# Attention and a gated feed-forward layer on one core: all probability-times-value products from the sixth pair on in 64x64 tiles, one drain copy per pair, a new order

## The chip, the cores and the metric

The kernel runs on one core of one Trainium2 chip. The metric is the device time of one execution in microseconds, lower is better. Three runs of the kernel before gave 418.28 us (median; 417.99 to 421.44). One execution was profiled: it took 417.28 us, of which 415.5 us lie between the start of its first and the end of its last profiled instruction (the span).

## The reference

```python
# q, k, v: (8, 12, 448, 64) float32; tau = 0.1
q_n = q / (norm(q, axis=-1) + 1e-6);  k_n = k / (norm(k, axis=-1) + 1e-6)
scores = q_n @ k_n.T / tau
attn = exp(scores - max(scores));  attn = attn / (sum(attn) + 1e-9)
x = (attn @ v).transpose(0, 2, 1, 3).reshape(8 * 448, 12 * 64)
# w_in: (768, 2048), w_out: (2048, 768)
h = x @ w_in
out = (h * cos(h)) @ w_out                   # (3584, 768) float32
```

## The kernel before, in words

**Work.** There are 8 batches of 12 heads. Two heads make a pair `g` (48 pairs, 6 to a batch), three pairs a unit `u`. For each pair the raw q and k rows are loaded by SyncE's queue, squared (`square`), summed over the head (`reduce`), turned into inverse norms (`rnorm`), scaled to bf16 (`scale`) and transposed (`transposes`, by TensorE for the first nine pairs, by DMA later). No maximum is taken out of the scores: cosine scores over tau are bounded.

**Scores.** `scores(g, c)` makes the transposed scores, keys on partitions, in 64x64 tiles of TensorE: 448 keys are seven blocks of 64, so block `c = 0` is half as wide (224 columns per matmul) and `c = 1, 2, 3` hold two blocks each (448 columns). ScalarE's exponential writes them in bf16 to `PH` (c = 0) and `PX` (c = 1 to 3).

**Gather.** `attend(g)` multiplies these probabilities by v and by ones (for the sums of the softmax) into one of three PSUM buffers (`AV`, `SC0`, `SC1`). It has two forms. The common form uses tiles of 128 rows by 32 columns: 12 matmuls of 448 columns at L979 (`av`), 4 of 224 at L1004 (`sm2`), 4 to 12 of 224 at L996 (`sm`), and the half block in 64x64 tiles at L972 (`row`). The other form, for the seven pairs listed in `PLAN["quarters"]` (7 to 11, 17 and 23), uses 64x64 tiles only: `run_phase` (L1015, `phase`) runs through the keys twice, once per diagonal of the tiles, each step being four matmuls of 224 columns in the four quadrants at once, and `ends` (L1024) does the half block. VectorE may first add `PX` blocks together (`FO`, "fold", L933), so that fewer matmuls with ones are needed; `folds(g)` says how many.

**Normalising.** For the pairs in `PLAN["direct"]` ScalarE makes exp(-ln(sum)) and GpSimd multiplies (L1077). For the others two copies drain the buffer (L1110 by VectorE, L1107 by ScalarE: 128x224 sums, then 128x448 values), and per unit `chain(u)` gathers the sums by DMA (`sums<-xu`), takes the reciprocal on VectorE (L1156), writes it to HBM (`scr<-rcp`), reads it back to all partitions (`RB<-scr`) and lets GpSimd multiply (L1163). The result `xT` is the transposed input of the next layer. The drained values stand in a ring of three units.

**Feed-forward layer.** Per batch `m1(b)` makes 16 blocks of h in 128x128 tiles (L1178); for each two blocks ScalarE takes the cosine (L1209) and VectorE multiplies (L1211) into `gT`. `m2_quarters` makes the output in rows of 128 with 64x64 tiles (L1278), the last ones `m2_fill` with 128x128 tiles (L1307). VectorE drains them (L1245).

**Order.** Everything is recorded as operations with reads and writes (`Program.op`); `arrange` plans all engines with estimated costs, per-operation biases (`PLAN["bias"]`) and, for TensorE, the order written out in `PLAN["order"]`. `PLAN["script"]` says when each score block (`s`), half block (`a`, `b`), values (`c`), first diagonal (`d`), batch (`m`) and filling of output work (`f`) is recorded. On the chip each engine then works through its own list in order and waits on semaphores. `P.settled(first, then)` marks an accumulation that must wait until an earlier matmul into the same columns has been written.

Of the kernel before, what the change touches and what calls it, by code (L numbers as in the profile page):

```python
# [6 lines left out]
ACT = mybir.ActivationFunctionType  # L7
# [11 lines left out]
    "vector": (20, 22, 24, 26, 32, 38, 40, 44, 46),  # L19
    "fold": 1,  # L20
    "folds": {6: 2, 8: 2, 10: 0, 12: 0, 16: 2, 17: 1, 18: 2, 20: 2, 21: 2, 22: 2, 24: 2, 25: 2, 26: 2, 27: 2, 30: 2,
# [12 lines left out]
    "v3": (7, ("xa", 2, 0)),  # L34
    "late4": {2: (7, "T9")},
    "power": (2,),
    "late": {6: 7.5, 9: 1.0, 11: 2.5, 13: 1.5},
# [10 lines left out]
    "scaled": {},  # L48
    "squared": {(5, 2): "A"},
# [5 lines left out]
    "direct": (0, 1, 2, 3, 4, 5, 7, 8, 9, 10, 11, 17, 23, 47),  # L55
# [196 lines left out]
class Program:  # L252
# [12 lines left out]
    LANDING = 0.45  # L265
    BOTH = 1.09
    COLD = 2.7
    ROOM = 2200

    def __init__(self, new_sem):  # L270
        self.new_sem = new_sem
# [8 lines left out]
    def op(self, eng, fn, reads=(), writes=(), cost=0.0, mode=None, dma=None, bulk=0.0, lock=False, label="", bias=0.0):  # L280
        o = Op()
# [1277 lines left out]
```

## Time and profile before

| What | us | Share of the span |
|---|---|---|
| Profiled execution | 417.28 | |
| Its span | 415.5 | |
| TensorE matmuls (PE) | 402.9 | 97% |
| Weight loads (PEld, beside PE) | 247.4 | 60% |
| VectorE (DVE) | 247.5 | 60% |
| ScalarE (ACT) | 261.7 | 63% |
| GpSimd (POOL) | 243.3 | 59% |

A busy time is the union of an engine's instructions. Matmuls overlap and their ends are modelled, so in the timeline the distance from one group's start to the next group's start tells what a group costs, not its length. "PE L1015 ... x4" is a group of four matmuls of line 1015.

### The profile page before, as it was taken

The numbers are of one execution on the slowest core, as the hardware profiler recorded it, in microseconds if no ns is written. First come the engines' busy times: TensorE is split into PE (matmuls) and PEld (weight loads), VectorE is DVE, ScalarE is ACT, GpSimd is POOL, SyncE is SP. The second block draws the span as 40 slices with busy tenths as digits, with TensorE's granted clock in tenths as the row PEclk, the third lists the DMA queues.
The fourth block names the chain that finished last, engine by engine and source line by source line (L and its number), as shares of the span: only waits on it lengthen the run. The fifth ranks groups of instructions, "written<-read, shape, count | busy, mean of one in ns | idle before, by whom it ended". The sixth has DMA issues, their size and how long they took to land.

```text
span 415.5 us, 13714 instructions
## 1 busy us (share of the span) xinstructions
PE 402.9 (97%) x6096; PEld 247.4 (60%) x6096; DVE 247.5 (60%) x350; ACT 261.7 (63%) x366; POOL 243.3 (59%) x192
## 2 busy tenths in 40 slices
PE   7899998999999999999899999999999999999997
PEld 3454556865667656765466657675566656655565
DVE  4564766357786598777674478454886555414412
ACT  5887577895888636876387656765486755413500
POOL 4999976799656675778657358816878300230000
PEclk9999999999999999999999999999999999999999
DMA  8999999869969998759945991989974800430114
GB/s 194 258 256 226 209 216 188 198 138 202 171 112 171 202 242 162 110 138 162 254 92 109 213 256 25 182 131 225 233 136 83 185 4 5 109 96 24 39 38 115
DMA packets 78591, 63.50 MB, mean 153 GB/s; under 512 B 43332, under 2 KB 73540, under 8 KB 78532
## 3 DMA queue, kind: packets, MB, share of 16 engines
q1 hardware_dynamic: 60324, 49.94, 57.7%
q0 software_dynamic: 18048, 12.59, 20.7%
q8 instruction: 48, 0.79, 0.8%
q10 hardware_dynamic: 160, 0.10, 0.1%
q14 instruction: 11, 0.09, 0.1%
HBM read 54.98 MB, written 11.13 MB: 159 GB/s over the span
## 4 chain that ended last, share of the span: by engine, by line
PE 86%; DMA 6%; POOL 3%; DVE 2%; ACT 1%; issue 1%; SPq 1%; DVEq 0%; POOLq 0%
PE MP L1278 26%; PE SC L1178 19%; PE AV L1178 9%; PE SC L914 5%; PE MP L1178 4%; PE MP L1307 4%; PE SC L979 3%; PE SC L1307 3%; PE AV L979 2%; DMA sums<-xu 2%; PE AV L1015 2%; DMA RB<-scr 1%; DMA scr<-rcp 1%; PE AV L914 1%; POOL qks L860 1%; DMA raw<-in_q_dram 1%
## 5 line engine op out<-in xcount | busy, mean ns | idle before, releaser
L1278 PE MATMUL MP<-W,gT 64*64 64x384 bf16 x2816 | 138.1, 323 | 1.8 <-issue 1.3
L929 ACT ACTIVATE PX<-SC 128x896 bf16<-128x896 f32 x115 | 102.4, 916 | 18.1 <-PE SC L914 17.0
L1278 PEld LDWEIGHTS MP<-W,gT 64*64 64x64 bf16 x2816 | 90.5, 107 | 25.5 <-issue 3.0
L860 POOL TENSOR_TENSOR qks<-raw,rn 128x896 bf16<-128x896 f32 (+1 forms) x48 | 80.2, 1680 | 26.1 <-ACT rn L852 16.5
L1178 PE MATMUL SC<-xT,W 128*128 128x448 bf16 x456 | 92.7, 353 | 1.8 <-DVE gT L1211 1.8
L822 POOL TENSOR_TENSOR sq<-raw 128x896 bf16<-128x896 f32 x44 | 73.6, 1684 | 20.8 <-DVE n L829 11.8
L1163 POOL TENSOR_TENSOR xT<-xu,RB 128x448 bf16<-128x448 f32 x34 | 38.0, 1136 | 66.8 <-DMA RB<-scr 47.1
L1178 PEld LDWEIGHTS SC<-xT,W 128*128 128x128 bf16 x456 | 44.0, 98 | 44.3 <-issue 3.2
L1209 ACT ACTIVATE cosb<-SC,cst 128x896 f32<-128x896 f32 x38 | 38.1, 1006 | 40.2 <-PE SC L1178 36.0
L829 DVE TENSOR_REDUCE n<-sq 128x14 f32<-128x896 bf16 (+2 forms) x49 | 51.3, 1056 | 4.5 <-ACT sq L820 4.1
L1211 DVE TENSOR_TENSOR gT<-SC,cosb 128x896 bf16<-128x896 f32 x38 | 41.1, 1086 | 20.4 <-ACT cosb L1209 17.9
L933 DVE TENSOR_TENSOR FO<-PX 128x896 bf16<-128x896 bf16 x39 | 37.8, 968 | 25.6 <-ACT PX L929 25.4
L1178 PE MATMUL AV<-xT,W 128*128 128x448 bf16 x228 | 47.7, 352 | 0.6 <-POOL xT L1163 0.6
L914 PE MATMUL SC<-qkT 64*64 64x448 bf16 x460 | 41.9, 357 | 0.6 <-ACT PX L929 0.4
L1209 ACT ACTIVATE cosb<-AV,cst 128x896 f32<-128x896 f32 x19 | 19.1, 1007 | 36.5 <-PE AV L1178 35.1
L1245 DVE COPY osb<-MP 128x384 f32<-128x384 f32 x50 | 25.8, 552 | 19.5 <-PE MP L1278 14.7
L1178 PEld LDWEIGHTS AV<-xT,W 128*128 128x128 bf16 x228 | 22.1, 98 | 21.4 <-ACT PX L929 1.1
L1211 DVE TENSOR_TENSOR gT<-AV,cosb 128x896 bf16<-128x896 f32 x19 | 20.7, 1090 | 22.5 <-ACT cosb L1209 22.5
L929 ACT ACTIVATE PX<-AV 128x896 bf16<-128x896 f32 x29 | 26.7, 920 | 6.2 <-PE AV L914 6.2
L796 POOL DMA_DIRECT2D va<-in_v_dram x32 | 21.8, 690 | 6.7 <-DMA raw<-in_q_dram 4.1
L929 ACT ACTIVATE PH<-SC 128x448 bf16<-128x448 f32 x37 | 20.2, 546 | 6.3 <-PE SC L922 5.3
L933 DVE TENSOR_TENSOR FO<-FO,PX 128x896 bf16<-128x896 bf16 x25 | 18.7, 749 | 6.4 <-ACT PX L929 5.4
(119 smaller groups left out, 470.3 us busy)
## 6 DMA issues: line engine op xcount, KB each, us to landing
raw<-in_k_dram SPq DMA_DIRECT2D x48, 224.0 KB, 6.3
raw<-in_q_dram SPq DMA_DIRECT2D x48, 224.0 KB, 7.1
out_dram<-osb SPq DMA_DIRECT2D x54, 192.0 KB, 3.4
va<-in_v_dram POOLq DMA_DIRECT2D x32, 192.0 KB, 7.1
RB<-scr SPq DMA_DIRECT2D x18, 336.0 KB, 4.9
W<-in_moe_w_in_dram POOLq DMA_DIRECT2D x4, 768.0 KB, 13.4
W<-in_moe_w_out_dram POOLq DMA_DIRECT2D x4, 768.0 KB, 16.3
RB<-scr SPq DMA_DIRECT2D x6, 224.0 KB, 3.5
```

The lines of the kernel that those rows point to most:

```text
L822: pool(lambda e, x=x, y=y: e.tensor_tensor(y, x, x, ALU.mult), src_, dst, 0.1 + n * 1.78e-3, label="sq%d.%d" % (u, p)).pad = LATE if u > 1 ...
L829: dve(lambda e, w=w: e.tensor_reduce(out=n2v[i][:, 2 * p : 2 * p + 2, w], in_=sqv[p][:, :, w, :], axis=mybir.AxisListType.X, op=ALU.add), ...
L860: f = lambda e, s0=s0, s1=s1: e.tensor_tensor(qksv[i][:, p, s0:s1].rearrange("p s h d -> p h s d"), rawv[i][:, h, s0:s1, :], bass.AP(rn[i] ...
L914: m = e.matmul(ph[BP * o : BP * o + BP, a, 0:S], t[r, c - 1 + (NT3 + 1) * o, 0:BP], t[r, :, BP : 2 * BP], start=True, stop=True)
L929: act(lambda e: e.activation(PHv[g % 3] if c == 0 else PXv[j][:, c - 1], ph[:, :, 0:n], ACT.Exp, scale=1.0 / TAU), keys, [("PX", j, c) if ...
L933: dve(lambda e: e.tensor_tensor(FO[j].ap(), x, PXv[j][:, c - 1].rearrange("p a s -> p (a s)"), ALU.add), [("PX", j, c), ("PX", j, 1) if c ...
L1163: f = lambda e, p=p: e.tensor_tensor(xTv[b % 2][:, UP * i + p, :].rearrange("p (s o m) -> p s o m", s=NB, o=2), xuv[:, u % 3, p, :].rearra ...
L1178: t = e.matmul(ph[:, a, 0:S], W1v[:, order[c], 128 * n : 128 * n + 128], xTv[b % 2][:, order[c], :], start=(c == 0), stop=(c == NKC - 1))
L1209: act(lambda e, ph=ph, cz=cz: e.activation(cosv[cz], ph[:, :, 0:S], ACT.Sin, bias=cst.ap()[:, 0:1], scale=1.0), names(gi) + ["cst0"], [("c ...
L1211: dve(lambda e, ph=ph, cz=cz, gi=gi: e.tensor_tensor(gTv[:, 2 * gi : 2 * gi + 2, S * (b % 2) : S * (b % 2) + S], ph[:, :, 0:S], cosv[cz], ...
L1278: r = e.matmul(POH[b][x : x + 64, 0:HW], gTv[k, y, col + x : col + x + 64], W2v[k, y, HW * b : HW * b + HW], start=(y == 0 and h == 0), st ...
L1307: r = e.matmul(po[:, 0 : w[1] - w[0]], gTv[:, y, col : col + 128], W2v[:, y, w[0] : w[1]], start=(y == 0), stop=(y == NF - 1))
```

## The change

- Pairs 6 to 47 all use the 64x64 form. The tile forms of L972, L979 (from pair 6 on), L996 and L1004 go.
- The query halves of a score block now stand swapped for 64 of the 128 rows (the moving operand is read with another stride), so that the two diagonals read contiguous halves.
- Where `tailed(g)`, VectorE also adds the half block `PH` onto `FO`, and the ones part of `ends` goes.
- One copy of 128x896 drains a non-direct pair, by ScalarE for the pairs in `acts`, else by VectorE; the ring has two units instead of three; `gather`, `spread` and the reciprocal work on 96x28 instead of 128x21.
- Two diagonals may run in either order with the half block (`dac` or `adc`); every step of the first half is the one that the second half must settle behind.
- ScalarE takes 13 more of the squares and 17 output drains (`oacts`); VectorE takes three scalings and three multiplications (`fast`); pair 35 becomes direct.
- The planner gets a model of TensorE's instruction fetch, output tiles are recorded per batch (`m2_upto`), all biases, delays, the order and the script are new.

```diff
-    "quarters": (7, 8, 9, 10, 11, 17, 23),
+    "quarters": (6, 7, 8, ..., 47),
-    "fold": 1,
+    "fold": 2,
+    "tailed": 1,
-    "late": {6: 7.5, 9: 1.0, 11: 2.5, 13: 1.5},
+    "late": {2: 3.5, 4: 3.0, 5: 3.0, 6: 5, 7: 3.0, 8: 5.0, 9: 3.0, 10: 3.0, 11: 3.5, 12: 3.5, 13: 3.0, 14: 3.0, 15: 1.0},
-    "grain": 4,
-    "fast": (),
+    "grain": 2,
+    "fast": (27, 33, 42),
...
@@ scores
+                    x = t[r, :, BP : 2 * BP]
+                    if g >= PB:
+                        x = bass.AP(qkT[y], 64 * a * 2 * S + BP + HQ * o, [[2 * S, 64], [HQ - 2 * HQ * o, 2], [2 * BP, NB], [1, HQ]])
+                    m = e.matmul(ph[BP * o : BP * o + BP, a, 0:S], t[r, c - 1 + (NT3 + 1) * o, 0:BP], x, start=True, stop=True)
...
+        if g >= PB and tailed(g) and c == 1 + folds(g):
+            xt = FO[j].ap().rearrange("p (a s) -> p a s", a=2)[:, :, 0:SH]
+            dve(lambda e: e.tensor_tensor(xt, xt, PHv[g % 3], ALU.add), [("F", j), ("PH", g % 3)], [("F", j)], SH, lock=True,
+                label="tail%d" % g, bias=PLAN["bf"][1])
@@ attend
-                    m = e.matmul(av_[64 * a : 64 * a + 64, b, x], w, source(kind, c)[r, a, :, b, :], start=(h == 0 and c == 0 and kind == "V"),
+                    m = e.matmul(av_[64 * a : 64 * a + 64, b, x], w, source(kind, c)[r, a, SH * h : SH * h + SH], start=(h == 0 and c == 0 and kind == "V" and not swapped),
...
                 if h and n == 0:
                     P.settled(opened[g], o)
+                opened[g] = o
...
-                    for k in range(2):
+                    for k in range(1 if tailed(g) else 2):
                         opened[g] = P.op("PE", lambda e, k=k: ends(e, k), ...
...
+            slot = slotv[:, i, p]
+            if not direct:
+                to, src_ = slot.rearrange("p x (h s) -> p h x s", h=2), av_[:, :, 0:S].rearrange("p h (x s) -> p h x s", x=2)
+                if g in PLAN["acts"]:
+                    act(lambda e: e.activation(to, src_, ACT.Copy, bias=0.0), both_keys, [("xa", i, p)], 2 * S, label="xu%d" % g)
+                else:
+                    dve(lambda e: e.tensor_copy(to, src_), both_keys, [("xa", i, p)], 2 * S, label="xu%d" % g)
+                return
...
@@ chain
-        dma("SP", [lambda e: e.dma_start(sums[i].ap()[:, 0:w], bass.AP(xu, XS[i], [[32 * XW, 4], [w, 32], [1, w]]))],
-            [("xs", i, p) for p in range(n)], [("sums", i)], "sums%d" % i, 0.35,
+        dma("SP", [lambda e: e.dma_start(sums[i].ap()[0:rows, :],
+                                         bass.AP(xu, i * UP * 2 * S + UP * S, [[64 * XW, 2], [w, 16 * n], [1, w]]))],
+            [("xa", i, p) for p in range(n)], [("sums", i)], "sums%d" % i, 0.35,
...
@@ m2_drain
-        if ends and w[1] == DM:
+        if ends and w[1] == DM or (t, hf) in PLAN["oacts"]:
@@ new
+    def m2_upto(n):
+        while m2_queue and m2_queue[0][0] < n:
+            t = m2_queue[0][0]
+            banks[0], nhalf[0] = [(["PO"], PO), (["TP"], TPF)], 0
+            while m2_tile or m2_queue and m2_queue[0][0] == t:
+                m2_fill(2 if t in PLAN["flat"] else 2 * NF, t not in PLAN["flat"])
@@ Program.play, for a TensorE operation: blocks of 256 instructions, asked for some 50 before an edge
+                        asked += self.BLOCK
+                        usable[asked] = t + self.FETCH + min(self.SHARE * behind, 5.5)
...
+                        o.end += max(0.0, usable[edge] - t)
```

More of the change, by code (lines that the diff above doesn't have):

```diff
@@ L248 @@
     __slots__ = ("eng", "fn", "idx", "deps", "cost", "mode", "dma", "bulk", "lock", "label", "bias",
-                 "start", "end", "late", "weight", "guard", "pad", "descs", "lead", "free", "waits", "inc", "count", "pos", "dcount", "known", "nd")
+                 "start", "end", "late", "weight", "guard", "pad", "descs", "lead", "free", "waits", "inc", "count", "pos", "dcount", "known", "nd", "ins")
 class Program:
@@ L306, in order_only @@
     def order_only(self, first, then):
+        assert first.eng == then.eng
         then.deps.append((first, None))
@@ L940, in folds, with tailed @@
         return PLAN["folds"].get(g, PLAN["fold"])
+    def tailed(g):
+        return folds(g) and PLAN["tails"].get(g, PLAN["tailed"])
     opened, held, turned = {}, {}, set()
@@ L965, in rest @@
                     m = e.matmul(to, w, PHv[g % 3][r, a, :],
[L966 to L973 removed]
+                                 start=(n == 0), stop=False)
             return m
@@ L979, in av @@
                 t = e.matmul(av_[o : o + 32, 0, 0:S], vav[y][:, 2 * p + a, c + 1, d : d + 32], PXv[j][:, c, a, :],
-                             start=(c == 0 and swapped), stop=(c == NT3 - 1 and not swapped))
+                             start=False, stop=(c == NT3 - 1))
             return t
```

338 lines of the change are left out of this document (155 added, 183 removed), and 268 rows, old and new, of the table PLAN.

## The prediction

> **What bounds the kernel now.** I read the page first, then the timeline of TensorE around the instructions that go, then counts per line, then the waits. The page:
>
> ```profile
> span 415.5 us, 13714 instructions
> ...
> PE 402.9 (97%) x6096; PEld 247.4 (60%) x6096; DVE 247.5 (60%) x350; ACT 261.7 (63%) x366; POOL 243.3 (59%) x192
> ...
> q8 instruction: 48, 0.79, 0.8%
> ...
> PE 86%; DMA 6%; POOL 3%; DVE 2%; ACT 1%; issue 1%; SPq 1%; DVEq 0%; POOLq 0%
> ```
>
> TensorE is idle 12.6 us in all and holds 86% of the chain that ended last; every other engine is busy for under two thirds. So an edit is worth what it does to TensorE's list: columns, changes of tile shape, and waits. The execution took 417.28 us, 1.8 more than its span. I keep that 1.8 and make the sum against 417.28; the median of the runs, 418.28, lies 1.0 above it.
>
> Where the idle time lies shows in four stretches (columns: length, then busy time of PE, PEld, DVE, ACT, POOL with counts, clock, DMA share and GB/s):
>
> ```profile
> 0.00:34.00 34.00, 29.74 (x352) 14.70 (x353) 19.75 (x37) 26.54 (x51) 28.60 (x30) 1.00 1.08 236
> ...
> 55.00:87.20 32.20, 29.57 (x768) 22.89 (x769) 16.55 (x29) 27.57 (x44) 23.14 (x18) 1.00 1.00 193
> ...
> 105.40:143.90 38.50, 37.87 (x922) 25.69 (x922) 26.96 (x46) 32.13 (x46) 22.52 (x17) 1.00 0.96 160
> ...
> 188.40:208.70 20.30, 18.48 (x104) 9.22 (x104) 14.00 (x16) 10.00 (x10) 14.64 (x11) 1.00 1.23 207
> ```
>
> 4.3, 2.6, 0.6 and 1.8 us of TensorE's idle time are here: the start, and 5.1 us in three places behind it. The rest of the kernel is columns back to back at the full clock (1.00).
>
> **Tile shapes.** This is the timeline of TensorE around one pair in the old form (start, length, group):
>
> ```profile
> 60.43 0.38 PE L914 MATMUL SC<-qkT 64*64 64x448 bf16 x4
> 60.74 0.75 PE L979 MATMUL AV<-PX,va 128*32 128x448 bf16 x12
> 61.32 0.27 PE L1004 MATMUL AV<-PH,half 128*32 128x224 bf16 x4
> 61.42 0.27 PE L996 MATMUL AV<-FO,ones 128*32 128x224 bf16 x4
> 61.62 0.60 PE L914 MATMUL SC<-qkT 64*64 64x448 bf16 x8
> ```
>
> And a pair in the new form:
>
> ```profile
> 65.07 0.27 PE L1015 MATMUL AV<-PX,va 64*64 64x224 bf16 x4
> 65.17 0.27 PE L1015 MATMUL AV<-FO,ones 64*64 64x224 bf16 x4
> 65.26 0.27 PE L1015 MATMUL AV<-PX,ones 64*64 64x224 bf16 x4
> 65.36 0.27 PE L1024 MATMUL AV<-PH,va 64*64 64x224 bf16 x4
> 65.45 0.27 PE L1024 MATMUL AV<-PH,ones 64*64 64x224 bf16 x4
> 65.79 0.48 PE L1015 MATMUL AV<-PX,va 64*64 64x224 bf16 x12
> ...
> 66.30 0.36 PE L914 MATMUL SC<-qkT 64*64 64x448 bf16 x4
> 66.48 0.33 PE L1278 MATMUL MP<-W,gT 64*64 64x384 bf16 x4
> ```
>
> Start to start, a group of four with 224 columns costs 0.095 to 0.10 in either shape (65.07 to 65.45 in four steps; 61.32 to 61.42); I take 0.096. A score group of 448 columns costs 0.18 (66.30 to 66.48), one of L979 0.193 (60.74 to 61.32 in three). Going from the score group into the 32-wide shape took 0.31, so 0.12 is the change; coming back took 0.20 from L996, so 0.10. A change costs 0.11 on average.
>
> The old form's counts after the first five pairs, in the windows view restricted to one line each: L979, L996, L1004, L972, L1015, L1024, in this order (the number in brackets):
>
> ```profile
> 55.00:415.50 360.50, 26.54 (x420) 1.00 0.74 141
> 55.00:415.50 360.50, 9.95 (x180) 1.00 0.74 141
> 55.00:415.50 360.50, 9.20 (x136) 1.00 0.74 141
> 55.00:415.50 360.50, 17.82 (x136) 1.00 0.74 141
> 55.00:415.50 360.50, 11.14 (x280) 1.00 0.74 141
> 55.00:415.50 360.50, 2.96 (x56) 1.00 0.74 141
> ```
>
> With 8 and 12 more of pair 47 that is 796 matmuls of 224 columns, 199 groups, and 432 of 448, 108 groups: 199 x 0.096 + 108 x 0.193 = 39.9 us. The changed program has 1488 of the two diagonals and 248 of the half block, all of 224 columns: 434 groups, 41.7 us. **Columns: +1.8.** The form is not cheaper in itself: each sum with ones is made twice over half of the keys. Without the deeper folds (66 additions and 22 tails instead of 64 additions) it would be more still.
>
> Along the two instruction orders TensorE changes its shape 102 times before and 56 times after. **Shapes: -46 x 0.11 = -5.1.** By 0.10 and 0.12 per change the ends are -4.6 and -5.5.
>
> A rule speaks against small groups: the Trainium skill's "TensorE: Matmul & The Clock Gate" (Part 1, on the 56 ns gap) says that starts of matmuls never come closer than about 25 ns, however few the columns. By it 434 groups would take 43.4 us and the sum would end 1.7 later; the trace (0.095 per four, 24 ns each) stands a little below that floor, and the sum goes by the trace.
>
> **Settling.** The second half must wait until the first is written. Where nothing stands between, 65.45 to 65.79 took 0.34 instead of 0.096: 0.24 per place. In the new order the second half follows directly in 7 pairs (6, 8, 22, 29, 30, 41, 47), and with one group of 0.1 between in 4 more; before in one. **+6 x 0.24 + 4 x 0.1 = +1.9**; at least 0 where the wait was due anyway, at most 0.24 for each of 21 pairs with under 0.2 us between, +5.
>
> **Output work.** 128 matmuls of L1278 (32 groups) become 32 of L1307's kind, 384 columns either way: 0.
>
> **Waits that may go.** The largest in the middle of the kernel are these:
>
> ```profile
> 142.98 0.27 PE L996 MATMUL SC<-FO,ones 128*32 128x224 bf16 x4
> 143.87 0.35 PE L1178 MATMUL AV<-xT,W 128*128 128x448 bf16 x1 [0.63 <-POOL xT L1163]
> ```
>
> ```profile
> 200.40 0.29 DVE L1156 RECIPROCAL rcp<-sums 128x21 f32<-128x21 f32 x1 [4.03 <-DMA sums<-xu]
> 200.60 1.03 DVE L1211 TENSOR_TENSOR gT<-SC,cosb 128x896 bf16<-128x896 f32 x1
> ...
> 201.78 0.54 PE L1178 MATMUL SC<-xT,W 128*128 128x448 bf16 x2 [1.81 <-DVE gT L1211]
> ```
>
> In the second a reciprocal stood at the head of VectorE's list and waited 4.03 us for its sums, with the product that frees TensorE's buffer queued behind it. The changed plan lets this unit's gather be 5 us late instead of 0.5, so the reciprocal is placed further back. I take both waits as gone, **-2.4**; ends: 0 (they come back elsewhere) and -2.4.
>
> **Instruction fetch.** TensorE also stopped for its own instructions:
>
> ```profile
> 70.13 0.49 PE L1278 MATMUL MP<-W,gT 64*64 64x384 bf16 x6
> 71.97 0.51 PE L1278 MATMUL MP<-W,gT 64*64 64x384 bf16 x6 [1.34 <-issue]
> ```
>
> The page (queue q8: packets, MB, share) has 48 instruction packets for 12,192 matmuls and weight loads: one per 254. In 105.4 to 143.9 that is one in 5.3 us now; the changed order puts 1060 matmuls instead of 920 there, one in 4.6 us, at a DMA share of 0.96. In 55 to 87 (768 matmuls before, 807 after) it is one in 5.3 us, and there it stopped. The plan now counts these fetches. I take **-0.5**, for part of this stop; ends: -1.3 (it goes) and, with the denser lists, the loss of the third rival.
>
> **Other engines.** Two copies of 224 and 448 columns become one of 896, by VectorE for 18 pairs, by ScalarE for 15. ScalarE gains 15 of these, 13 squares and 17 output drains and loses 10 copies. The nearest rows:
>
> ```profile
> L929 ACT ACTIVATE PX<-SC 128x896 bf16<-128x896 f32 x115 | 102.4, 916 | 18.1 <-PE SC L914 17.0
> ...
> L822 POOL TENSOR_TENSOR sq<-raw 128x896 bf16<-128x896 f32 x44 | 73.6, 1684 | 20.8 <-DVE n L829 11.8
> ...
> L1211 DVE TENSOR_TENSOR gT<-SC,cosb 128x896 bf16<-128x896 f32 x38 | 41.1, 1086 | 20.4 <-ACT cosb L1209 17.9
> ...
> L933 DVE TENSOR_TENSOR FO<-PX 128x896 bf16<-128x896 bf16 x39 | 37.8, 968 | 25.6 <-ACT PX L929 25.4
> ```
>
> At 0.92 for each of 28 and half of it for the 17 drains less the 10 copies, ScalarE goes from 262 to about 291 us, 70%. GpSimd loses 13 x 1.68 of squares, three scalings and three multiplications and falls to about 213. VectorE loses about as much in copies as it gains in folds, tails, scalings and multiplications (18 copies at 1.09 are the largest gain) and stays near 247. None comes near TensorE: **0**, covered by their idle third. If that cover fails, it shows as the second rival.
>
> The gather moves 96 rows of 28 instead of 128 rows of 21, as many bytes on the same queue, and no DMA is added: 0. The ring of two units makes a drain wait for the multiplication two units back; I take 0, since a unit's first drain comes four pairs, some 17 us (38.5 us for the nine pairs of 105 to 144), after the last drain of the unit whose place it takes. The start is unchanged but for three more filler matmuls: 0, ends -2 (half of the 4 us that TensorE idles in the first 34 us) and +1.
>
> **Sum.** +1.8 - 5.1 + 1.9 - 2.4 - 0.5 = -4.3. 417.28 - 4.3 = **413.0 us**.
>
> **The rivals.** First: *the forecast*. TensorE stays the bound and works through a list shorter by 1.4 us of columns, shapes and settling, with 2.9 us less waiting.
>
> Second: *the sums arrive late*. The ones-group of the folded sums now waits for two additions and a tail on VectorE. For it: an addition takes 0.97 us on average and itself follows an exponential of 0.92, so the last of three is done some 3 us after the scores. Against it: VectorE has 40% of its time free, and two additions per pair stood in the old order without a long wait of TensorE among its 5.1 us. If 22 tailed pairs each cost TensorE 0.2 us, that is +4.4: 417.4, no change.
>
> Third, on the other side: *instruction fetch becomes the bound of the attention stretches*. For it: the stop above happened at one packet in 5.3 us, and the new stretches come to about 4.5. Against it: 105 to 144 ran at 5.3 and a DMA share of 0.96 with 0.6 us idle in all, so a density that stops is not yet shown. The attention stretches of the new order hold 4,800 matmuls, 38 packets. One stop of 1.34 in every fourth is 9.5 x 1.34 = 12.7: 425.7. It turns a gain into nothing from an average of 0.11 us per packet, and into over 1% slower than 418.28 from 0.25.
> The Trainium skill's "Runtime: NRT & Kernel Launch" (Instruction fetch mechanics) says that such fetches, in blocks of 256 instructions, are mostly hidden. By it this rival is void and the fetch term 0; the block size agrees with the 254 above, but the 1.34 us of the trace do not.
>
> **How the numbers follow.** Forecast 0.52; late sums 0.28; fetch 0.20. About 1% is what a measurement of this kernel can tell from no change; 1% below 418.28 is 414.1, and the forecast's own spread reaches over that line about as often as late sums turn out harmless. So faster 0.52, same 0.28, slower 0.20. The range: downwards all settling but 0.5 hidden (-1.4), the fetch stop gone (-0.8), shapes at 0.12 (-0.4), the start better by 2, and 1 for other idle time give 407.5; upwards it takes in late sums and five stops of 1.34 with one microsecond of settling, 420.5.
>
> **What would show it.** Right: no tile of 128x32 after pair 5; PE near 400 us busy and still 97% of the span; starts of the new groups 0.096 apart; ScalarE near 290; no wait of TensorE behind a reciprocal. Wrong: "issue" ahead of TensorE's groups at more than two places (fetch), TensorE idle behind VectorE's additions or behind drains (late sums), gaps of 0.3 us at most second halves (settling), or ScalarE on the chain.

## The result, and the profile after

The changed kernel took 420.28 us (median of 18 runs, 418.37 to 422.35), the kernel before beside it 417.87 (18 runs); the ratio is 1.0077, 95% interval 1.005 to 1.0103. The same kernel again, in a later series of runs (e9 below, "the control"), gave 419.79 and 1.0015 (0.998 to 1.005). So the change does not save the 4.3 us of the forecast; it costs between nothing and 1%. Each ratio here and below is against the kernel before in the same series, whose median went from 417.87 to 419.25 us, and leaves out the runs in a slower state. The profiled execution took 419.64 us, 2.4 more than the one before.

The page of the changed kernel, the same rows as those shown of before:

```profile
span 417.7 us, 14563 instructions
...
PE 405.9 (97%) x6511; PEld 255.7 (61%) x6511; DVE 242.6 (58%) x321; ACT 289.1 (69%) x403; POOL 217.8 (52%) x173
...
q8 instruction: 51, 0.84, 0.8%
...
PE 85%; ACT 4%; DVE 4%; DMA 3%; POOL 2%; issue 1%; SPq 0%; DVEq 0%; ACTq 0%; POOLq 0%
```

TensorE is busy for 3.0 us more, not for less, and ScalarE and VectorE together hold 8% of the chain instead of 3%. ScalarE's 289.1 us and GpSimd's 217.8 are near the forecast (291 and 213). The stretches that correspond to the four shown of before (length, busy time and count of PE, PEld, DVE, ACT, POOL, clock, DMA share, GB/s):

```profile
0.00:35.30 35.30, 31.54 (x355) 15.31 (x356) 18.40 (x33) 26.62 (x50) 29.14 (x31) 1.00 1.08 234
55.00:88.60 33.60, 32.04 (x817) 22.91 (x814) 16.86 (x28) 30.12 (x49) 22.50 (x14) 1.00 0.93 189
106.90:147.10 40.20, 38.47 (x1061) 30.75 (x1060) 24.98 (x34) 33.26 (x48) 23.48 (x18) 1.00 0.88 155
191.90:210.20 18.30, 18.30 (x100) 9.31 (x96) 13.67 (x16) 13.95 (x15) 9.08 (x9) 1.00 1.11 221
```

The last stretch, which held the reciprocal, is 2.0 us shorter and has no idle time left. The three ahead of it are 1.3, 1.4 and 1.7 longer. So one part of the forecast came true in full, and something else took it back.

To find it I went through TensorE's whole list in both traces, group by group: from the start of one group to the start of the next, less the time of its columns at the full rate (0.187 us for four tiles of 448), and put what was left under what the next group is: another tile shape, a second half that waits for its first, a group that waits for another engine, or a place where instructions ran out. The sums are differences of starts, so they add up to the whole (2.26 us between the two spans):

| Step of the forecast | forecast, us | found, us |
|---|---|---|
| Columns | +1.8 | +1.8 |
| Changes of shape (62 to 15 behind the start) | -5.1 | -5.3 |
| Settling, and small gaps between groups | +1.9 | +4.1 |
| Waits behind the reciprocal and xT | -2.4 | -2.6 |
| Instruction fetch | -0.5 | -0.1 |
| Other engines: exponentials +1.0, sums +1.3, drains +0.8 | 0 | +3.1 |
| Start, up to the first output product | 0 | +1.0 |
| End, behind the last matmul | 0 | +0.3 |
| Sum | -4.3 | +2.3 |

These are two profiles, one of each kernel. Which of the rows for gaps and for other engines a short stop belongs to depends on how it is sorted; some 0.7 us could stand in either. In the control's profile the start is +1.2, the stretch from the first output product to the last matmul 0.6 us shorter than in the first profile, and the sums are some 0.4 smaller.

**Settling.** A second half directly behind its first (start, length, engine, line, group):

```profile
173.59 0.29 PE L1057 MATMUL AV<-FO,ones 64*64 64x224 bf16 x4
173.71 0.27 PE L1066 MATMUL AV<-PH,va 64*64 64x224 bf16 x4
174.04 0.48 PE L1057 MATMUL AV<-PX,va 64*64 64x224 bf16 x12
```

From 173.71 to 174.04 is 0.34 us instead of 0.096, a stop of 0.245; a semaphore holds the second half until the last matmul of the first has been written. The same stop is 0.15 with a group of 0.1 between the halves and 0.055 with a score group of 0.19 between: work and stop always make about 0.25. In the changed list 29 places stop in this way, for 3.9 us; in the old one 20 places for 1.5. That is +2.4 of the +4.1; the rest is spread over gaps of a few ns at more than 2000 starts, and no run shows its cause.

**Sums.** VectorE and GpSimd, and what TensorE does with the result:

```profile
282.40 0.63 DVE L1175 TENSOR_TENSOR xT<-xu,RB 128x448 bf16<-128x448 f32 x1 [3.78 <-DMA RB<-scr]
...
283.70 1.57 POOL L1175 TENSOR_TENSOR xT<-xu,RB 128x448 bf16<-128x448 f32 x1 [2.33 <-DVE FO L993]
...
284.32 1.20 DVE L998 TENSOR_TENSOR FO<-FO,PH 128x448 bf16<-128x448 bf16 x1
```

```profile
285.58 0.29 PE L1057 MATMUL AV<-FO,ones 64*64 64x224 bf16 x4 [0.79 <-DVE FO L998]
```

The reciprocal no longer blocks VectorE. But pair 33's product, one of three that the new plan gives to VectorE, stands at the head of its list for 3.78 us until a broadcast lands; the additions of pair 38 are queued behind it, and TensorE waits for their tail. A wait of the same kind has come back a few stages later. Something else adds to it: the tail took 1.20 us instead of the usual 0.39. GpSimd's multiplication stood beside it until 285.27, and the tail ended 0.25 later. In this profile 18 of VectorE's 88 additions are long in this way, and each of the 18 ends 0.48 us (the tail 0.25) after the end of a GpSimd multiplication that was running when it began. Without that, the tail would have ended about 0.8 earlier (an estimate, 1.20 less 0.39), about when TensorE came to it.

**Exponentials and drains.** One example of each:

```profile
59.33 0.38 PE L975 MATMUL SC<-qkT 64*64 64x448 bf16 x4 [0.32 <-ACT PH L989]
...
77.28 0.60 PE L1066 MATMUL AV<-PH,va 64*64 64x224 bf16 x4 [0.20 <-DVE xu L1124]
```

**Fetch.** The second of the two stops of before (the first is shown in the prediction), and the largest of this profile:

```profile
77.37 0.29 PE L1015 MATMUL AV<-PX,va 64*64 64x224 bf16 x3 [0.72 <-issue]
```

```profile
139.37 0.28 PE L1057 MATMUL AV<-PX,va 64*64 64x224 bf16 x1 [1.31 <-issue]
```

The two stops of before (1.55 and 0.89 us from start to start) are gone, and 2.3 us stand in four places, the other three at 77, 115 and 191 us.

### The profile page after: what moved, and what is told of

It is laid out like the page before. It is cut to its first block, busy times and chain, and to the rows that moved or that the text cites. A ratio compares the mean times of both kernels' runs of the same rounds, so it can differ in the third digit from the quotient of the medians.

```text
span 417.7 us, 14563 instructions
## 1 busy us (share of the span) xinstructions
PE 405.9 (97%) x6511; PEld 255.7 (61%) x6511; DVE 242.6 (58%) x321; ACT 289.1 (69%) x403; POOL 217.8 (52%) x173
## 4 chain that ended last, share of the span: by engine, by line
PE 85%; ACT 4%; DVE 4%; DMA 3%; POOL 2%; issue 1%; SPq 0%; DVEq 0%; ACTq 0%; POOLq 0%
PE MP L1309 22%; PE SC L1209 21%; PE AV L1209 10%; PE MP L1338 5%; PE SC L975 5%; PE AV L1057 4%; PE MP L1209 4%; PE SC L1057 4%; PE SC L1338 3%; DMA RB<-scr 1%; ACT PX L989 1%; DMA scr<-rcp 1%; PE AV L975 1%; POOL qks L918 1%; PE SC L982 1%
## 5 line engine op out<-in xcount | busy, mean ns | idle before, releaser
L1209 PE MATMUL SC<-xT,W 128*128 128x448 bf16 x468 | 96.9, 353 | 0.0
L1309 PEld LDWEIGHTS MP<-W,gT 64*64 64x64 bf16 x2688 | 80.9, 107 | 24.3 <-issue 2.3
L918 POOL TENSOR_TENSOR qks<-raw,rn 128x896 bf16<-128x896 f32 (+1 forms) x45 | 75.2, 1681 | 31.7 <-ACT rn L910 14.2
L1175 POOL TENSOR_TENSOR xT<-xu,RB 128x448 bf16<-128x448 f32 x39 | 44.4, 1151 | 84.4 <-DMA RB<-scr 42.9
L880 POOL TENSOR_TENSOR sq<-raw 128x896 bf16<-128x896 f32 x31 | 52.0, 1693 | 11.0 <-DVE n L887 5.8
L993 DVE TENSOR_TENSOR FO<-PX 128x896 bf16<-128x896 bf16 x37 | 30.0, 811 | 32.6 <-ACT PX L989 32.4
L1209 PEld LDWEIGHTS AV<-xT,W 128*128 128x128 bf16 x216 | 20.7, 98 | 19.6 <-issue 0.9
L1276 DVE COPY osb<-MP 128x384 f32<-128x384 f32 x38 | 20.1, 553 | 21.2 <-PE MP L1309 12.3
L1338 PE MATMUL MP<-W,gT 128*128 128x384 bf16 x128 | 24.9, 326 | 0.0
L1057 PE MATMUL AV<-PX,va 64*64 64x224 bf16 x480 | 23.1, 258 | 1.7 <-issue 1.3
L1242 DVE TENSOR_TENSOR gT<-AV,cosb 128x896 bf16<-128x896 f32 x18 | 19.6, 1087 | 8.6 <-ACT cosb L1240 7.1
```

What stands on the lines that cost most here:

```text
L880: pool(lambda e, x=x, y=y: e.tensor_tensor(y, x, x, ALU.mult), src_, dst, 0.1 + n * 1.78e-3, label="sq%d.%d" % (u, p)).pad = LATE if u > 1 ...
L918: f = lambda e, s0=s0, s1=s1: e.tensor_tensor(qksv[i][:, p, s0:s1].rearrange("p s h d -> p h s d"), rawv[i][:, h, s0:s1, :], bass.AP(rn[i] ...
L1057: m = e.matmul(av_[64 * a : 64 * a + 64, b, x], w, source(kind, c)[r, a, SH * h : SH * h + SH], start=(h == 0 and c == 0 and kind == "V" a ...
L1175: f = lambda e: e.tensor_tensor(x, a, r, ALU.mult)
L1209: t = e.matmul(ph[:, a, 0:S], W1v[:, order[c], 128 * n : 128 * n + 128], xTv[b % 2][:, order[c], :], start=(c == 0), stop=(c == NKC - 1))
L1242: dve(lambda e, ph=ph, cz=cz, gi=gi: e.tensor_tensor(gTv[:, 2 * gi : 2 * gi + 2, S * (b % 2) : S * (b % 2) + S], ph[:, :, 0:S], cosv[cz], ...
```

## The experiments

All of them keep the plan of the kernel that they start from: an edit moves single instructions in an engine's list, or changes what one instruction does, after everything has been planned. In the short diffs, put(engine, label, n, front, k) takes the n-th operation of a label out of its engine's list and puts it ahead of the k-th operation of another; SC, R and AV are score, half-block and product groups of a pair, M2 output work of a tile. "Less stops" below means: from the first output product to the last matmul, without the stops for instructions, which differ from run to run. It is 353.2 us for the kernel before, 354.2 and 353.5 in two profiles of the changed one, each good to about 0.1.

**e1, the first ten us.**

```diff
+    put("ACT", "ln0.0b", 0, "sq0.1", 0)
+    put("ACT", "rn0.0b", 0, "sq0.1", 0)
+    put("DVE", "scale0.0", 0, "red0.1", 0)
```

> The changed kernel with three instructions moved on two engines, nothing else: on ScalarE the logarithm and exponential for the second part of the first pair's norms go ahead of the squares of the second pair, on VectorE the scaling that needs them goes ahead of the second pair's reduction, as both stood in the kernel before. In the changed kernel's profile that scaling began at 9.52 us instead of 7.54, the first scores at 10.91 instead of 10.30 and the first product with W at 35.25 instead of 33.94. Theory: this order is what the start lost; the first product comes back to 34.0 to 34.6 and the whole to 419.3 to 419.8 (from 420.28). Rival: the start is set by the arrival of the loads and by the new order of TensorE's list, so the first product stays at 35.2 and the time at 420.3.

419.5 us, ratio 1.0035 (1.0003 to 1.0066). Timeline of TensorE, first scores and first product with W:

```profile
10.50 0.29 PE L982 MATMUL SC<-qkT 64*64 64x224 bf16 x4
...
35.34 0.55 PE L1209 MATMUL MP<-xT,W 128*128 128x448 bf16 x2
```

The scores came 0.4 earlier, the product did not. The rival holds for the start: these three instructions are not what it lost. The time of 419.5 lies where the theory put it, but the control came to 419.79 without any edit.

**e2, eight gaps filled.**

```diff
+    put("PE", "SC6.2", 0, "M2 0", 6)
+    put("PE", "M2 0", 11, "AV6", 4)
+    put("PE", "SC24.0", 0, "AV22", 4)
+    put("PE", "M2 10", 3, "AV27", 4)
+    put("PE", "M2 11", 4, "AV29", 4)
+    put("PE", "M2 18", 4, "AV41", 3)
+    put("PE", "M2 18", 5, "AV41", 4)
+    put("PE", "M2 23", 3, "AV47", 4)
```

> The changed kernel with eight groups moved on TensorE's list, nothing else: groups of output work or scores that stood behind a second half go ahead of it, in pairs 6, 22, 27, 29, 41 and 47 and in the first output tile, so that the first half is written by the time the second begins. In the changed kernel's profile TensorE stood still for 0.248, 0.524, 0.245, 0.147, 0.245, 0.150, 0.261, 0.286, 0.269 and 0.246 us at these places, 2.6 us. Theory (settling and late sums are paid in full, since TensorE is the bound): the stops go and the time falls by 2.0 to 2.6, to about 418. Rival (TensorE only waits there for what other engines would have held it for anyway): the next waits for ScalarE and VectorE grow by as much and the time stays within 0.6 of 420.3.

419.12 us, ratio 1.0019 (0.9991 to 1.0048). The stops of second halves fell from 3.9 to 1.9 us, and the stretch less stops from 354.2 to 353.7. Three of the waits that came instead:

```profile
60.87 0.29 PE L982 MATMUL SC<-qkT 64*64 64x224 bf16 x4 [0.28 <-ACT PX L989]
...
172.31 0.29 PE L982 MATMUL SC<-qkT 64*64 64x224 bf16 x4 [0.29 <-ACT PX L989]
...
317.60 0.29 PE L982 MATMUL SC<-qkT 64*64 64x224 bf16 x4 [0.25 <-DVE xu L1117]
```

These score groups had started without a long wait; now TensorE comes to them before the exponential or the drain that frees their buffer. Of the 2.0 us taken away at most a quarter reached the end (354.2 and 353.5 for the unchanged list): in the trace the rival holds, and the time, 0.7 to 1.2 below the changed kernel's two medians, doesn't decide against it.

**e13, twelve gaps opened.** The same question the other way round.

```diff
+    put("PE", "AV15", 5, "M2 4", 7)
+    put("PE", "AV16", 5, "M2 4", 12)
...
+    put("PE", "AV39", 4, "M2 17", 0)
```

> The changed kernel with twelve groups moved on TensorE's list, nothing else, against the direction of the run that filled the gaps: in pairs 7, 15, 16, 17, 18, 20, 21, 25, 26, 36, 38 and 39 the first group of the second half, which stood behind output work of 0.32 us or more, goes ahead of it, directly behind the first half. In the changed kernel's profiles such a group waits 0.245 us with nothing between, 0.15 with a group of 0.1, 0.055 with one of 0.19 and 0.00 to 0.005 at these twelve. Theory (each such wait is TensorE's own, and half of it is given back by later waits, as where the gaps were filled): twelve new stops of 0.24, 2.9 us in all, and the stretch from the first output product to the last matmul, less the stops for instructions, longer by 1.2 to 2.0 (354.2 in the first profile of the changed kernel, 353.5 in the control). First rival (paid in full): by 2.5 to 2.9. Second rival (settling is covered, the loss of the forecast lies elsewhere): by less than 0.7.

421.0 us, ratio 1.0079 (1.0049 to 1.0109): 0.7 and 1.2 above the changed kernel's two medians, by the ratios 0 to 2.7, so the time alone decides nothing. One of the twelve places:

```profile
131.07 0.27 PE L1066 MATMUL AV<-PH,ones 64*64 64x224 bf16 x4
131.41 0.29 PE L1057 MATMUL AV<-PX,va 64*64 64x224 bf16 x4
```

The stops of second halves rose by 3.0 us, and the stretch less stops came to 357.4, 3.2 and 3.9 more than in the two profiles of the unchanged list. In the trace the first rival holds: new settling is paid in full, and a little more; the wait for pair 38's tail, for one, rose from 0.79 to 1.24. The profiled execution, 424.22 us, was the slowest of the six, so this rests on one trace. It speaks against the half price that was expected after e2, and for another reading of e2: settling is on the path, but taking it away gives little back, because the next engine is close behind.

**e3, the product that blocked VectorE.**

```diff
+    put("DVE", "fold38", 0, "x33", 0)
+    put("DVE", "fold38", 1, "x33", 0)
+    put("DVE", "tail38", 0, "x33", 0)
```

> The changed kernel with one instruction moved on VectorE: pair 33's product, which stood at the head of VectorE's list for 3.78 us until its broadcast had landed at 282.40 us, goes behind pair 38's two additions and its tail. In the changed kernel's profile TensorE waited 0.79 us (0.96 counted from start to start) at 285.58 for that tail. Theory: a wait for a transfer at the head of VectorE's list is what made the sums late, as the reciprocal did in the kernel before; TensorE's stop at 285.6 falls to under 0.2 and the time by 0.6 to 0.9. Rival: the sums are late because of their own length of two additions and a tail behind an exponential; the stop stays above 0.6 and the time at 420.3.

419.0 us, ratio 1.0022 (0.9992 to 1.0052). TensorE at the place, and 31 us later:

```profile
284.91 0.27 PE L1057 MATMUL AV<-FO,ones 64*64 64x224 bf16 x4
...
315.82 0.29 PE L1057 MATMUL SC<-FO,ones 64*64 64x224 bf16 x4 [0.40 <-DVE FO L998]
```

The stop is gone and the product with W behind it started at 286.00 instead of 286.70. The control shows how much of this is luck: there the broadcast landed sooner and the same product started at 285.96 without an edit.

```profile
281.64 0.63 DVE L1175 TENSOR_TENSOR xT<-xu,RB 128x448 bf16<-128x448 f32 x1 [2.98 <-DMA RB<-scr]
```

Start to start, the stop behind pair 38's tail is 0.96 us in the first profile and 0.18 in the control, 0.49 to 1.48 in seven of the variants that leave this order alone, and 0.00 in the two that move the product (e3 and e11). So the theory holds for the place, though its price differs from run to run. For the time it does not: less stops, the stretch to the end is 353.9, inside the two of the unchanged list. Where pair 38's stop is short, the sums of pair 41 can wait longer: 0.57 here and in the control, 0.29 in the first profile.

**e4, the reciprocal, in the kernel before.**

```diff
+    put("DVE", "recip", 4, "g3.4", 0)
```

> The kernel before with one instruction moved on VectorE: the reciprocal that waited 4.03 us for its sums, until 200.40 us, goes behind the next two products of the activation and two reductions; this is the part of the change that the sum priced at -1.8 of its -2.4, done alone. Theory: TensorE's wait of 1.81 us at 201.78 goes and nothing takes its place, 417.9 falls to 415.9 to 416.3. Rival: the time is given back within a few us (by the broadcast that now lands later, or by a fetch), and the time stays at 417.4 to 418.2.

416.01 us, ratio 0.9945 (0.9921 to 0.997): faster by 2.3, a little more than the theory gave. The runs of the kernel before in that series went from 415.68 to 423.65, these from 414.71 to 418.15. VectorE, and TensorE in the place of the wait of 1.81:

```profile
201.03 0.28 DVE L1156 RECIPROCAL rcp<-sums 128x21 f32<-128x21 f32 x1
```

```profile
198.67 3.76 PE L1178 MATMUL SC<-xT,W 128*128 128x448 bf16 x19
```

The sums have landed when the reciprocal's turn comes, and TensorE runs through. This term of the forecast was right, and it needs nothing of the rest of the change.

**e5, the tile shape undone.**

```diff
-                    m = e.matmul(av_[64 * a : 64 * a + 64, b, x], w, source(kind, c)[r, a, ...
+                    m = e.matmul(av_[32 * q : 32 * q + 32, 0, x], w, source(kind, c)[:, a, ...
```

> The changed kernel with the tile shape undone and nothing else: every group of four 64x64 matmuls of the pairs from the sixth on becomes four of 128x32, also of 224 columns, in the same place of the same list with the same waits; the groups of a pair then add into one bank, so what comes out is not attention (and three activations are scaled to stay finite). Columns are equal; along the list the changes of shape rise from 54 to 306. Theory of the prediction (0.11 us per change, paid in full): +252 x 0.11 = +27.7, about 448. Rival (most changes hide behind waits that are there anyway, so the change's gain of 5.1 never was one): under +14, below 434.

441.89 us (2 runs), 21.6 more than the changed kernel's 420.28; by the two ratios (1.0547 and 1.0077) it is 19.6. The new groups, by form:

```profile
L1059 PE MATMUL SC<-PX,va 128*32 128x224 bf16 x528 | 23.0, 263 | 0.3
L1059 PE MATMUL AV<-PX,va 128*32 128x224 bf16 x480 | 22.2, 263 | 0.2
```

21.6 over 252 changes is 0.086 us each, four fifths of the 0.11 that the sum used. The trace says where the fifth went. From start to start the 252 changes cost 27.9 us, 0.111 each, just what the theory has, and the other stops fell by 6.5: those for instructions from 2.3 to none, the waits for other engines from 4.6 to 0.9, the stops of second halves from 3.6 to 2.4 (counted here only where the trace names the semaphore that ended the wait), while small gaps rose by 0.7. So a change is paid in full and a slower TensorE wins some of it back, because the others are then ready when it comes. The theory was closer than the rival, and the new order, which puts scores and output work between almost all groups, is affordable only with one shape.

**e6, short drains.**

```diff
+                if g > 17 and g != 29:
+                    to, src_ = to[:, :, :, 0:32], src_[:, :, :, 0:32]
...
+        m = 64 if t > 5 else n
```

> The changed kernel with its drain copies cut short and nothing else: from pair 18 on (but 29) each copy of a pair's products takes 32 of 224 columns, and from tile 6 on each copy of output takes 64 of 384, so most of the output is left out; ScalarE and VectorE each lose some 20 us of work behind 125 us, TensorE's list and all waits stay. Theory (what the prediction set at 0 under other engines is real: VectorE's and ScalarE's turn comes late): TensorE's waits behind tails, drains and exponentials behind 125 us, some 2.2 us in the changed kernel's profile, fall to under 0.7 and the time to 417.5 to 419. Rival (these are latencies of chains, not of busy engines): they stay above 1.5 us and the time at 419.5 to 420.5.

419.61 us, ratio 1.0038 (0.9994 to 1.0083). The edit took 17 us off VectorE and 12 off ScalarE. TensorE's waits behind 125 us fell from 2.1 to 0.9 us, the time did not fall. Neither theory's figures came (under 0.7, above 1.5), and the fall is not shown to come from the edit: the control has 1.3 and e8, whose drains are whole, 0.9. One that is left:

```profile
287.01 0.29 PE L1057 MATMUL AV<-FO,ones 64*64 64x224 bf16 x4 [0.32 <-DVE FO L998]
```

This is pair 38's tail again, behind the same product on VectorE:

```profile
283.81 0.63 DVE L1177 TENSOR_TENSOR xT<-xu,RB 128x448 bf16<-128x448 f32 x1 [3.89 <-DMA RB<-scr]
```

In e8 the same stop is as long (0.32). The broadcast blocks VectorE however short its other work, so this place hangs on a chain; for the other places the run does not tell load from chains. The stops for instructions came to 4.7 us in this profile, so for the time itself the run tells little.

**e7, short stores.**

```diff
-            ... [[NB * DM, BP], [1, c1 - c0]]), osb[o].ap()[p0 : p0 + BP, c0:c1]) ...
+            ... [[NB * DM, BP], [1, (c1 - c0) // 6]]), osb[o].ap()[p0 : p0 + BP, c0 : c0 + (c1 - c0) // 6]) ...
```

> The changed kernel with every store of output cut to a sixth of its columns (most of the output isn't written) and nothing else: the transfers that stand beside the instruction packets become fewer, the number of instructions is the same. Theory (TensorE stops for instructions when the packet lands late behind other transfers): the stops for instructions, 2.3 us in the changed kernel's profile and 4.0, 1.9 and 2.5 in those of its three variants, fall to under 1 and the time by 1 to 2.5, to 418 to 419.3. Rival (the packets wait for broadcasts and loads, or the density of instructions alone decides): stops of 1.9 to 4 us remain, the time stays within 0.6 of 420.

418.43 us, ratio 0.9974 (0.9934 to 1.0014), with no run of the unedited list beside it. The stops for instructions came to 1.9 us, and the largest stood where it did in the first profile:

```profile
139.94 0.28 PE L1057 MATMUL AV<-PX,va 64*64 64x224 bf16 x1 [0.86 <-issue]
```

The time speaks for the theory, the profile for the rival. What holds the packets up stays open.

**e8, the old opening.**

```diff
+    for e, text in (("PE", """TP0 TP0 SC0.0 SC0.1 SC0.2 TP1 TP1 SC0.3 SC1.0 SC1.1 ..."""), ("ACT", ...
+        for o, t in zip(first, sorted(o.start for o in first)):
+            lanes[e].remove(o)
+            o.start = t
+        lanes[e][at:at] = first
```

> The changed kernel with the order of the opening undone and nothing else: up to the first product with W, TensorE, ScalarE, VectorE and GpSimd take their instructions in the order of the kernel before (the opening has the same operations in both; three more filler products stay). In the profiles of the changed kernel and its three variants that product starts at 35.17 to 35.34, in those of the kernel before at 33.94 and 34.09. Theory (the new order of the opening costs 1.0 to 1.3 us, which no single instruction of the first ten us explains): it starts at 33.9 to 34.4, the first output tile at 56.4 to 56.8 instead of 57.5, and the time falls by 1. Rival (the start is set by the loads, or by the three fillers): it stays above 34.9.

420.3 us, ratio 1.0005 (0.9965 to 1.0044), with stops for instructions of 5.2 us in its profile; a fall of 1 us can't be seen. The first product with W here:

```profile
34.80 0.55 PE L1209 MATMUL MP<-xT,W 128*128 128x448 bf16 x2
```

In e11, with the same opening, it started at 34.36. With the new order it stood at 35.17 to 35.46 in nine profiles and at 36.42 in that of e7, in the kernel before and its variants at 33.94 to 34.27. So the old order gives back 0.5 and 0.9 of a loss of some 1.2; the rest goes with the three fillers or the loads and was not separated.

**e9, the control.** No edit.

> The changed kernel once more, without an edit, as a control beside the others. In eight profiles of lists that differ from the changed kernel's in a few places only, TensorE's stops for instructions came to 1.9 to 5.2 us. Theory (the stops hang on how the transfers happen to fall, so they differ from run to run of one program): they come to something else than the 2.3 us of its first profile, at the same places (77 to 92, 139 and 191 us), and the median lies between 419 and 420.5. Rival (the stops are fixed by the list, and the edits moved them): 2.3 us again, within 0.3.

419.79 us, ratio 1.0015 (0.998 to 1.005). Two of its stops:

```profile
78.64 0.29 PE L1066 MATMUL AV<-PH,va 64*64 64x224 bf16 x3 [0.89 <-issue]
...
139.47 0.28 PE L1057 MATMUL AV<-PX,va 64*64 64x224 bf16 x1 [0.37 <-issue]
```

The sum is 2.4 again, as the rival said, but not the single stops: start to start, the stop at 139 fell from 1.51 to 0.57 and the one at 78 rose from 0.23 to 1.06, in the same program.

**e10, two edits in the kernel before.**

```diff
+    put("DVE", "recip", 4, "g3.4", 0)
...
+            for y in range(y0, y0 + m) if t in (1,) else ():
+                r = e.matmul(POH[h][:, 0:HW], gTv[:, y, col : col + 128], W2v[:, y, HW * h : HW * h + HW], ...
```

> The kernel before with two edits: the reciprocal moved as in the run of that alone (which gave 416.0), and the second tile of output work made of 128x128 matmuls instead of 64x64: the same columns in the same places of the list, a quarter of the instructions, 288 less between 66 and 78 us, and 10 more changes of shape. In both profiles of that kernel's list so far TensorE stopped there for instructions for 1.55 and 0.89 us. Theory (too many instructions per us for the fetch): both stops go, the changes cost 10 x 0.1 = 1.0, the time is 1.0 to 1.5 below the 416.0 of the reciprocal alone, 414.5 to 415. Rival (the stops are set by other transfers, not by the number of instructions): they stay above 1.5 us in all and the time rises to 417.

415.57 us, ratio 0.9905 (0.9869 to 0.9941), against 0.9945 for the first edit alone. In the place of the two stops:

```profile
71.03 0.66 PE L1275 MATMUL MP<-W,gT 128*128 128x384 bf16 x3
71.62 0.38 PE L914 MATMUL SC<-qkT 64*64 64x448 bf16 x4
71.84 0.46 PE L1015 MATMUL AV<-PX,va 64*64 64x224 bf16 x12
72.12 0.27 PE L1015 MATMUL AV<-FO,ones 64*64 64x224 bf16 x4
72.32 1.47 PE L1275 MATMUL MP<-W,gT 128*128 128x384 bf16 x8
...
268.22 0.84 PE L1283 MATMUL MP<-W,gT 64*64 64x384 bf16 x14 [1.75 <-issue]
```

Both stops are gone, and the stretch from the first output product to the second feed-forward block is 29.0 us instead of the 30.8 of e4, after paying for ten changes of shape. Fewer instructions took away these two stops, which both profiles of the list with small tiles have. But a stop of 1.92 us (start to start) stands at 268 us in this profile, where e4 had 0.35 and the kernel before none, so over the whole kernel the stops fell only from 2.8 to 2.2. This is the lowest median of the study, though its interval overlaps that of e4; it has nothing of the change but a better place for one reciprocal.

**e11, three edits together in the changed kernel.** The edits of e2, e3 and e8.

> The changed kernel with three of the earlier edits together: the eight groups moved into the gaps, pair 33's product behind pair 38's tail, the opening in its old order. Theory (settling, sums behind a blocked VectorE and the opening each cost what their stretches showed: 0.95, 0.65 and 0.45): 2.0 below the unchanged list of the same call, 417.5 to 418.5. Rival (they give back to each other and to the fetch): within 0.8 of it.

418.08 us, ratio 0.9996 (0.996 to 1.0032): 1.7 below the control by the medians, 0.8 by the ratios, so the two theories are not told apart by the time. The first output product starts 1.1 earlier than in the control; less stops the rest is as long as there (353.4), with a new wait of 1.2 us for pair 36's drain at 278 us. What was won is the start.

**e12, one whole tile in the changed kernel.** The edit of e10 for the seventh tile, `t in (6,)`.

> The changed kernel with one tile of output work, between 130 and 147 us, made of 128x128 matmuls instead of 64x64: the same columns in the same places, a quarter of the instructions, 22 more changes of shape. In all seven profiles of this list and its variants TensorE stopped for instructions at 139 to 141 us, for 0.53 to 1.51. Theory: the stop goes (-1.0) and the changes cost 0.09 to 0.11 each (+2.0 to +2.4), so the stretch from 107 to 147 us grows by 0.9 to 1.4 and the time by 1 to 1.4. Rival (changes are hidden here): the stretch shrinks by 1.

420.99 us, ratio 1.0045 (1.0014 to 1.0076), 0.3% over the control of the same series. Around 139 us:

```profile
138.12 0.50 PE L1306 MATMUL MP<-W,gT 128*128 128x384 bf16 x2
138.55 0.29 PE L1057 MATMUL SC<-FO,ones 64*64 64x224 bf16 x4
...
138.87 0.50 PE L1306 MATMUL MP<-W,gT 128*128 128x384 bf16 x2
139.30 0.29 PE L1057 MATMUL AV<-PX,va 64*64 64x224 bf16 x4
139.52 0.50 PE L1306 MATMUL MP<-W,gT 128*128 128x384 bf16 x2
```

No stop, and each block of output work now costs a change on either side. The stretch from 106.9 us is 40.9 long with 0.4 of stops left at 115, against 40.2 and 38.6 in the two profiles of the unchanged list with 1.9 and 0.6: less stops 2.2 and 2.4 longer for 22 changes, 0.10 to 0.11 each. The price holds, and the time rose by 1.2 us as the theory said; the stretch itself grew by 0.7 and 2.3, not by 0.9 to 1.4, since the stops of the unchanged list differ between its two profiles.

## Why the prediction was wrong

The direction was wrong: 413.0 forecast, 419.8 to 420.3 measured. Of the 6.6 us between the two sums of the table, other engines make 3.1, settling and gaps 2.2, the start 1.0 and the end 0.3. The time lies inside the range (407.5 to 420.5), at its edge, and nearest to the second rival's 417.4. That it lies inside is partly luck: the upper end was added up from five stops for instructions and one microsecond of settling (which gives 420.7), and that is not what happened. Of the forecast's signs of being right PE near 400 failed (405.9); of its signs of being wrong idle time behind additions and drains came, and ScalarE on the chain (4%).

**Columns: right.** +1.8, as forecast. The starts of the new groups are 0.095 apart, so the Trainium skill's floor ("TensorE: Matmul & The Clock Gate", Part 1) doesn't show in this trace: four matmuls start within 0.095, 24 ns each, where that section says about 25.

**Shapes: right.** -5.3 against -5.1. e5 puts 252 changes in and its trace pays 0.111 for each (0.086 net), e12 puts 22 in and pays 0.10 to 0.11.

**Settling: mis-sized, the first failure.** +1.9 stood in the sum, +4.1 was found, +2.4 of it as stops. The price of 0.24 was right (0.245). What failed in the stops is the count: "the second half follows directly in 7 pairs, with one group of 0.1 between in 4 more". Work and stop make 0.25 together, so every place with less than that between the halves stops: 9 places for 0.22 to 0.27, 5 for about 0.15, 15 for 0.055 to 0.08, second halves of output tiles among them, which the sum left out. The other 1.7 are short gaps between groups, for which the sum had no term; their cause stays open. In e13's trace such stops are paid in full where they are put in.

**Other engines: 0, the second failure and the largest.** +3.1 was found: exponentials, tails and drains that TensorE waits for, in many places of 0.1 to 1.0 us. The step argued from busy shares, "none comes near TensorE". Its 0.97 us for an addition was an average, too: in the profile of before 23 of 64 additions are long, nearly all beside a GpSimd instruction, and the short ones take 0.63. But e2 shows that where TensorE is made faster it meets a buffer that is not yet free within a few us, and e5 the reverse: with TensorE slowed by 27.9 us these waits fall from 4.6 to 0.9. At pair 38's tail the wait comes from a blocked head of VectorE's list and from GpSimd's multiplication beside the tail, not from load; for the other places e6 leaves it open. Busy shares under two thirds did not mean cover. This is the second rival's mechanism, though not its form: not 22 tails at 0.2 us, but one or two large ones and several exponentials and drains.

**Waits that go: right.** -2.6 against -2.4, and e4 shows the larger of the two alone. But the plan's three products on VectorE brought in a new wait of 3.78 us behind a broadcast; the step looked only at the wait removed, not at what else the plan puts at the head of VectorE's list.

**Fetch: about right, badly known.** In ten profiles of the changed list and of edits that keep its number of instructions the stops came to 1.9 to 5.2 us, in the kernel before to 2.4 and 2.8. The third rival (12.7 us) did not come. The Trainium skill's "Runtime: NRT & Kernel Launch" (Instruction fetch mechanics) has such fetches mostly hidden. The trace agrees so far: 51 packets took some 56 us (0.8% of 16 engines' span), and TensorE stood still for 2.3 of it. What it stood still for depends on the run, so that -0.1 came near -0.5 is luck; e10 shows two stops cured and another come.

**Start: 0, the third failure.** +1.0. "The start is unchanged but for three more filler matmuls" overlooked that the opening's order was new on four engines; e8 and e11 give 0.5 and 0.9 of it back.

## What to carry to other kernels

A tile shape that saves switches can be worth its full price and still bring nothing, as here, if the order that it allows brings as many short waits: count every place where an accumulation is reopened less than the settling time after its last write, not only the direct neighbours. In this kernel, with one engine 97% busy, the others were only a few tenths of a us behind; price a gain at the engine by what the next buffer allows, and look at what stands at the head of each queue behind a transfer. Test single terms in the old kernel first: here one instruction moved gave 2.3 us, and a quarter of the instructions for one tile took away both stops for fetching there, if not the one that came elsewhere.

## What the runs showed of the hardware that was not expected

The stops for instructions are no property of the list alone. The same program stopped for 1.51 us at 139 us in one execution and for 0.57 in another, with 0.23 and 1.06 at 78 us. Reopening an accumulation costs 0.22 to 0.27 us from the end of the last write's columns where nothing or little stands between (nine places of the first profile, five of them at 0.245 or 0.246). VectorE's bf16 additions seem to wait for a GpSimd instruction that is running when they begin: the tail of pair 38 took 1.20 to 1.21 us in ten profiles instead of 0.39, each time beside GpSimd's multiplication. In e11 the addition ahead of it met that multiplication, took 1.50 instead of 0.62, and the tail took 0.40. In the first profile and the control all long additions (18 and 19 of 88) end 0.48 us, a tail 0.25, after the end of a GpSimd multiplication. No run tests it by an edit of its own.
